# Moving the D parts of the hidden tiles beside the second layer, and splitting half of w2 earlier in the second group

## The chip, the cores and the metric

The kernel runs on one core of one Trainium2 chip. The metric is the device time of one execution in microseconds (us).

## The reference

The kernel computes a gated linear recurrence, and feeds its result to four small networks (experts) whose outputs are mixed with given probabilities.

```python
# q, k, v, alpha: (4, 8, 768, 48)
for t in range(S):
    state = alpha[:, :, t, :, None] * state + einsum('bhd,bhe->bhde', k[:, :, t], v[:, :, t])
    y[:, :, t] = einsum('bhd,bhde->bhe', q[:, :, t], state)
x = y.transpose(0, 2, 1, 3).reshape(3072, 384)
p = domain_probs / (domain_probs.sum(-1, keepdims=True) + 1e-09)     # (3072, 4)
for e in range(4):
    h = maximum(x @ w1[e], 0)            # w1: (4, 384, 1024)
    out += p[:, e:e + 1] * (h @ w2[e])   # w2: (4, 1024, 384)
```

All inputs and outputs are float32.

## The kernel before

**Blocks and groups.** The 3072 rows are 24 blocks of 128 rows. Group 0 has two blocks, groups 1 to 5 have four each, group 6 has two. The blocks' recurrence ("attention" below) is computed chunk by chunk on all engines, in small steps; the expert networks of a group run on TensorE meanwhile. The main loop runs over (group, expert) pairs; in the end groups 5 and 6 alternate expert by expert. The order of all instructions is written out by hand: each engine takes its own in the order in which the program issues them. The attention steps of a later group are dealt out over the earlier group's work by a clock of estimated costs (`cost`, `advance`, `deal`), so that a group's input is ready a little ahead of its first layer.

**First layer (`up`).** For each of the eight hidden tiles `fc` of an expert, the 128 hidden features of all the group's rows (512 columns, in group 6 256) are computed. From group 1 on, x and w1 are split in three float32r parts: a top part T, a low part L (the rest) and a D part, a fixed combination of T and L. Six matmuls (parts T and L) go to the PSUM tile `one` and three (part D) to `two`. ScalarE scales `one` into `t` (line 551), VectorE adds `two`. In groups 0 and 1 a rectified whole float32 tile is then written (lines 558 and 594). From group 2 on `hidden_parts` makes the three parts of the hidden tile: ScalarE writes T (line 578), VectorE L (line 580), and VectorE D = T/4096 - L (`make_dif`, line 590) in two halves of 256 columns. The first half of D is made at once; the second is put into the queue `later`, and is made in the second layer, one at every fourth step. Tiles are finished one tile late: the T and L of a tile are issued after the next tile's matmuls.

**Second layer (`down`).** For a block (128 columns of the hidden tiles as stationary operand, 384 columns of w2 as moving one) eight hidden tiles are summed in PSUM. In groups 0 and 1 this is done in full float32, one block a turn (line 628, one sum). From group 2 on it is done in parts, two blocks a turn: 48 matmuls a turn, first T and L of tiles 0 to 5 for both blocks, then T and L of tiles 6 and 7, and D last; T and L go to one sum and D to another (line 624), so that a turn takes four PSUM banks. `add_up` (line 658) scales the sums by the block's probability and adds them to `acc`. PSUM's tag "g" has four banks, shared by `one`, `two` and these sums.

**Weights.** In group 0 w1 pieces, and in group 1 w2 pieces, are split by `split_piece` (four pieces an expert; two ScalarE and two VectorE instructions each, lines 224 to 230), and the parts are stored to DRAM (`kept`, line 231, from POOL's queue). Later groups load the parts from there (line 195, SP's queue). In groups 0 and 1 the whole w2 pieces are loaded beside the first layer into unused parts of the hidden tiles (line 215, SP's queue); in group 1 pieces 0 and 1 are loaded at hidden tile 0 and pieces 2 and 3 at tile 2. Group 1's splits are issued during its second layer: `background` takes each piece one step on at every call, in `down` twice a turn, in `up` once a hidden tile.

Of the kernel before, what the change touches and what calls it, by code (L numbers as in the profile page):

```python
# [10 lines left out]
F32 = mybir.dt.float32  # L11
# [9 lines left out]
def kernel(  # L21
# [37 lines left out]
    nc = tc.nc  # L59
# [79 lines left out]
    splitting = []  # L139
    stores = deque()  # L140
    late = deque()
    later = deque()
    shared = {}
    accs = {}

# [6 lines left out]


    split1 = lambda gi, e: gi > 0
    split2 = lambda gi, e: gi > 1
    makes = [lambda gi, e: gi == 0, lambda gi, e: gi == 1]


# [28 lines left out]
    def load_piece(l, i, beside=False):  # L187
        if i >= E * NQ * LAST:
            return
        gi, k = divmod(i, E * NQ)  # L190
        e, c = divmod(k, NQ)
        if (split1, split2)[l](gi, e):
            w = wt[l][i] = wts.tile([P, 3, KC * QF], F32R, name=f"w{l + 1}",
                                    bufs=AHEAD if l == 0 else NQ)
            nc.sync.dma_start(out=w.bitcast(F32), in_=kept[l][k])
            return
        if l == 1 and not beside:
            return
        if l == 0:

            if gi > 0 or e == 0:
                shared[c] = wts.tile([P, 3, KC * QF], F32R, name="w2", bufs=NQ)
            w = shared[c][:, 2 - e % 2 if gi == 0 else 2].bitcast(F32)
        else:

            w = hidden[c][:, 0].rearrange("p f n -> p (f n)")[:, :KC * QF].bitcast(F32)
        wt[l][i] = w
        if l == 0:
            heads = moe_w1[e].rearrange("(h d) f -> h d f", d=D)[:, :, c * QF:(c + 1) * QF]
            w = w.rearrange("p (c f) -> p c f", f=QF)  # L210
            for part in range(2):
                nc.sync.dma_start(out=w[:, part], in_=heads[part * H // 2:(part + 1) * H // 2, :QUAD])
            nc.sync.dma_start(out=w[:, 2], in_=heads[:, QUAD:])
        else:
            nc.sync.dma_start(
                out=w.rearrange("p (c d) -> p c d", d=DM),
                in_=moe_w2[e].rearrange("(c p) d -> p c d", p=P)[:, c * FPQ:(c + 1) * FPQ])

    def split_piece(l, i):
        whole = wt[l][i]  # L220
        w = wts.tile([P, 3, KC * QF], F32R, name=f"w{l + 1}", bufs=AHEAD if l == 0 else NQ)
        top, low, dif = (w[:, part] for part in range(3))

        nc.scalar.activation(out=top, in_=whole, func=ACT.Copy, scale=TRIM)
        yield
        nc.scalar.activation(out=dif, in_=whole, func=ACT.Copy, scale=TRIM * 4096)
        yield
        nc.vector.scalar_tensor_tensor(out=low, in0=whole, scalar=4096.0, in1=dif.bitcast(F32),
                                       op0=ALU.mult, op1=ALU.subtract)
        nc.vector.tensor_sub(dif, low.bitcast(F32), top.bitcast(F32))  # L230
        nc.gpsimd.dma_start(out=kept[l][i % (E * NQ)], in_=w.bitcast(F32))
        if l == 0:
            del wt[0][i]

    def background():

# [266 lines left out]
    def up(gi, e, fc, slots=None):  # L503
# [5 lines left out]
        if fc == 0 and begins:  # L509
            for k in range(NQ):  # L510
                hidden[k] = hid.tile([P, 3, FPQ, NT], F32R, name="hT", bufs=NQ)
        if fc in ((0, 2) if gi == 1 else (0,)) and begins and not split2(gi, e):
            half = range(fc, fc + 2) if gi == 1 else range(NQ)
            for k in half:
                load_piece(1, (gi * E + e) * NQ + k, beside=True)
        if makes[0](gi, e) and ends and fc in SPLIT_AT[e in (0, E - 1)]:
            k = SPLIT_AT[e in (0, E - 1)].index(fc)
            making.append(split_piece(0, (gi * E + e) * NQ + k))
# [11 lines left out]
        if not split1(gi, e):  # L530
            for kc in range(KC):
                nc.tensor.matmul(one, lhsT=w[:, kc], rhs=xraws[gi][:, kc, lo:hi],  # L532
                                 start=(kc == 0), stop=(kc == KC - 1))
            nc.scalar.activation(out=whole, in_=one, func=ACT.Relu)
        else:
            two = ps.tile([P, NT], F32, name="two", tag="g", bufs=4)[:, :n]
            for out, terms in ((one, (1, 0)), (two, (2,))):
                for part in terms:
                    for kc in range(KC):
                        nc.tensor.matmul(out, lhsT=w[:, part, kc], rhs=x_part(gi, part, kc),  # L540
                                         start=(part == terms[0] and kc == 0),
                                         stop=(part == terms[-1] and kc == KC - 1))

            ends_first = gi < LAST
            for steps in finish:
                for _ in steps if ends_first else [next(steps)]:
                    pass
            ahead = [] if ends_first else list(finish)
            finish.clear()
            t = work.tile([P, NT], F32, name="t")[:, :n]  # L550
            nc.scalar.activation(out=t, in_=one, func=ACT.Copy, scale=FINE)  # L551
            if split2(gi, e):
                nc.vector.tensor_add(t, t, two)  # L553
                for steps in ahead:
                    next(steps, None)
                finish.append(hidden_parts(t, parts))
            else:
                nc.vector.tensor_add(whole, t, two)  # L558
                finish.append(rectified(whole))
# [16 lines left out]
    def hidden_parts(x, parts):  # L576
        top, low, dif = parts
        nc.scalar.activation(out=top, in_=x, func=ACT.Relu, scale=TRIM)  # L578
        yield
        nc.vector.scalar_tensor_tensor(out=low, in0=x, scalar=0.0, in1=top.bitcast(F32),  # L580
                                       op0=ALU.max, op1=ALU.subtract)

        n = x.shape[-1]
        at = n // 2 if n == NT else 0
        if at:
            make_dif(*(part[:, :at] for part in parts))
        later.append([part[:, at:] for part in parts])

    def make_dif(top, low, dif):
        nc.vector.scalar_tensor_tensor(out=dif, in0=top.bitcast(F32), scalar=1 / 4096.0,  # L590
                                       in1=low.bitcast(F32), op0=ALU.mult, op1=ALU.subtract)
# [5 lines left out]
    def down(gi, e, slots, between):  # L597
# [2 lines left out]
        first = first_piece(gi, e)  # L600
        halves_ = split2(gi, e)
        if slots[0] == 0 and makes[1](gi, e):
            making.extend(split_piece(1, first + k) for k in range(NQ))
        if slots[0] == 0 and makes[0](gi, e) and 0 < e < E - 1:
            making.extend(split_piece(0, first + k) for k in range(2, NQ))
        sums = [[ps.tile([P, DM], F32, name=f"ops{j}", tag="g", bufs=4)
                 for j in range(2 if halves_ else 1)] for _ in slots]

        kinds = [((0, 1), range(FCH - 2)), ((0, 1), range(FCH - 2, FCH)), ((2,), range(FCH))]
        steps = [(part, i, fc) for parts, tiles in (kinds if halves_ else [((3,), range(FCH))])  # L610
                 for part in parts for i in range(len(slots)) for fc in tiles]
        for n, (part, i, fc) in enumerate(steps):
            c, f = divmod(fc, FPQ)
            h = hidden[c][:, :, f, slots[i] * P:(slots[i] + 1) * P]
            advance(cost(1, gi, e) / FCH / (3 if halves_ else 1))
            while between and n >= between[0][0] * len(steps):
                between.popleft()[1]()
            if n == len(steps) // 2:
                background()
            if later and n % 4 == 3:  # L620
                make_dif(*later.popleft())
            if halves_:
                w = wt[1][first + c].rearrange("p t (c d) -> p t c d", d=DM)[:, part, f]
                nc.tensor.matmul(sums[i][part // 2], lhsT=h[:, part], rhs=w,  # L624
                                 start=(fc == 0 and part != 1), stop=(fc == FCH - 1 and part != 0))
            else:
                w = wt[1][first + c].rearrange("p (c d) -> p c d", d=DM)[:, f]
                nc.tensor.matmul(sums[i][0], lhsT=h[:, 2].bitcast(F32), rhs=w,  # L628
                                 start=(fc == 0), stop=(fc == FCH - 1))
            if part >= 1 and fc == FCH - 1:  # L630
                add_up(gi, e, slots[i], part // 2, sums[i][part // 2 if halves_ else 0])
        while between:
            between.popleft()[1]()
        background()
# [35 lines left out]
    def cost(layer, gi, e):  # L670
        n = len(groups[gi]) / 4
        if layer == 0:
            return 2.1 * n if split1(gi, e) else 2.6 * n
        return 4.1 if split2(gi, e) else 5.4

    def deal():

# [29 lines left out]
    def advance(spent):  # L707
        nonlocal clock
        clock += spent
        while waiting and clock >= waiting[0][0]:  # L710
            next(waiting.popleft()[2], None)
# [96 lines left out]
```

## Time and profile before

| | |
|---|---|
| time, median of 3 runs | 1072.71 us (1072.09 to 1073.56) |
| the profiled execution's own time | 1073.32 us |
| its span in the profile | 1071.6 us |
| granted TensorE clock | 0.998 of full speed |
| busy: PE, PEld, DVE, ACT, POOL | 98%, 84%, 72%, 53%, 3% |

PE is TensorE's matmuls, PEld its weight loads, DVE is VectorE, ACT ScalarE, POOL GpSimd; SP issues most of the DMAs. The stages lie in the span as follows (read off the timeline of TensorE, start of the first layer and of the second):

| stage | first layer from | second layer from | next from |
|---|---|---|---|
| group 1, expert 0 | 165.4 | 187.6 | 215.9 |
| group 1, expert 1 | 215.9 | 236.9 | 261.3 |
| group 1, expert 2 | 261.3 | 283.3 | 306.7 |
| group 1, expert 3 | 306.7 | 329.0 | 352.4 |
| group 2, expert 0 | 352.4 | 374.8 | 394.2 |
| group 4, expert 3 | 818.9 | 841.8 | 862.0 |
| group 5, expert 1 | 914.6 | 931.1 | 948.1 |
| group 6, expert 1 | 948.1 | 957.1 | 965.5 |

The rows of the profile's views are explained where they are shown.

### The profile page before, as it was taken

How to read it: one execution, taken by the hardware profiler on the slowest of the kernel's cores; microseconds unless marked ns; L12 is line 12 of the kernel's file. 1: busy time of each engine (PE TensorE's matmuls, PEld its weight loads, DVE VectorE, ACT ScalarE, POOL GpSimd, SP SyncE). 2: the span in 40 equal slices, each digit the busy share in tenths (PEclk: the TensorE clock that was granted, in tenths of full speed). 3: DMA queues.
4: the chain of work that ended last, by engine and by line, in shares of the span. 5: the costliest groups of instructions: out<-in, count | busy, mean ns of one | idle time of the engine just before them, and what ended most of it. 6: DMA issues, size and time to landing. Idle time of an engine off the chain costs nothing.

```text
span 1071.6 us, 21614 instructions
## 1 busy us (share of the span) xinstructions
PE 1048.1 (98%) x8460; PEld 899.1 (84%) x8460; DVE 775.2 (72%) x1711; ACT 566.7 (53%) x1202; POOL 32.7 (3%) x71
## 2 busy tenths in 40 slices
PE   8899999999999999999999999999999999999998
PEld 8777777676776798898898898898889889898988
DVE  5488776656566978778877777986787866666565
ACT  5687866575656554536546445555464543323232
POOL 2010000000000100000000000000000000000000
PEclk9999999999999999999999999999999999999999
DMA  8597699687696967758759558586594543544540
GB/s 123 156 330 216 230 328 368 238 328 241 236 309 209 402 216 274 281 160 312 268 170 359 204 187 337 186 281 234 158 358 173 221 192 147 207 177 178 187 181 31
DMA packets 158838, 251.67 MB, mean 235 GB/s; under 512 B 120112, under 2 KB 135344, under 8 KB 136208
## 3 DMA queue, kind: packets, MB, share of 16 engines
q1 hardware_dynamic: 149600, 208.82, 57.1%
q0 software_dynamic: 5760, 41.29, 9.8%
q8 instruction: 67, 1.10, 0.4%
q10 hardware_dynamic: 3376, 0.17, 0.3%
q14 instruction: 35, 0.29, 0.1%
HBM read 207.79 MB, written 42.47 MB: 234 GB/s over the span
## 4 chain that ended last, share of the span: by engine, by line
PE 83%; DVE 8%; ACT 6%; issue 2%; DMA 1%; SPq 0%; DVEq 0%; ACTq 0%
PE ops L624 25%; PE one L540 21%; PE ops L628 10%; PE two L540 10%; PE sc L334 6%; PE yps L428 3%; PE tp L266 3%; PE one L532 2%; ACT qb L308 2%; PE far L389 1%; PE sps L463 1%; DVE near L344 1%; DVE t L553 1%; DVE hT L580 1%; DVE hT L590 1%
## 5 line engine op out<-in xcount | busy, mean ns | idle before, releaser
L624 PE MATMUL ops<-w,hT 128*128 128x384 f32 x1728 | 318.0, 339 | 4.4 <-DVE acc L658 4.3
L624 PEld LDWEIGHTS ops<-w,hT 128*128 128x128 f32 x1728 | 299.1, 188 | 9.9 <-DVE acc L658 5.6
L540 PE MATMUL one<-xT,w 128*128 128x512 f32 x960 | 253.8, 400 | 2.6 <-DVE xT L248 1.1
L540 PEld LDWEIGHTS one<-xT,w 128*128 128x128 f32 x960 | 176.3, 188 | 41.8 <-DVE QT L315 1.6
L551 ACT ACTIVATE t<-one 128x512 f32<-128x512 f32 (+1 forms) x192 | 106.3, 554 | 153.6 <-PE one L540 148.5
L308 ACT COPY qb<-QT 64x256 f32<-64x256 f32 x336 | 136.4, 406 | 77.0 <-DVE QT L289 44.1
L578 ACT ACTIVATE hT<-t 128x512 fp32r<-128x512 f32 (+1 forms) x160 | 94.3, 589 | 123.6 <-DVE t L553 122.9
L580 DVE SCALAR_TENSOR_TENSOR hT<-t,hT 128x512 fp32r<-128x512 f32 (+1 forms) x160 | 102.2, 638 | 55.7 <-ACT hT L578 53.6
L540 PE MATMUL two<-xT,w 128*128 128x512 f32 x480 | 136.7, 393 | 0.0
L628 PE MATMUL ops<-hT 128*128 128x384 f32 x384 | 133.4, 491 | 0.0
L553 DVE TENSOR_TENSOR t<-t,two 128x512 f32<-128x512 f32 (+1 forms) x160 | 100.8, 630 | 41.9 <-ACT t L551 21.4
L590 DVE SCALAR_TENSOR_TENSOR hT<-hT 128x256 fp32r<-128x256 f32 x288 | 111.9, 422 | 4.4
L540 PEld LDWEIGHTS two<-xT,w 128*128 128x128 f32 x480 | 90.6, 189 | 20.0
L628 PEld LDWEIGHTS ops<-hT 128*128 128x128 f32 x384 | 69.5, 190 | 40.1 <-issue 0.4
L315 DVE TENSOR_TENSOR QT<-QT,dec 128x256 f32<-128x256 f32 x144 | 60.8, 422 | 38.2 <-ACT qb L308 37.5
L344 DVE COPY_PREDICATED near<-masks,sc 128x256 f32<-128x256 uint8 x144 | 77.0, 535 | 15.5 <-PE sc L334 12.8
L334 PEld LDWEIGHTS sc<-qb,KT 128*64 128x64 f32 x2304 | 72.7, 138 | 9.7 <-issue 5.6
L334 PE MATMUL sc<-qb,KT 128*64 128x64 f32 x2304 | 77.2, 223 | 2.6 <-ACT qb L308 2.6
L658 DVE SCALAR_TENSOR_TENSOR acc<-ops,p_all,acc 128x384 f32<-128x384 f32 x82 | 49.5, 614 | 33.9 <-PE ops L624 14.5
L326 ACT COPY KT<-KT 128x256 f32<-128x256 f32 x144 | 59.9, 416 | 3.2
L327 DVE TENSOR_TENSOR KT<-KT,dec 128x256 f32<-128x256 f32 x144 | 60.3, 419 | 0.0
L558 DVE TENSOR_TENSOR hT<-t,two 128x512 f32<-128x512 f32 x32 | 22.0, 688 | 35.6 <-ACT t L551 23.0
(88 smaller groups left out, 970.7 us busy)
## 6 DMA issues: line engine op xcount, KB each, us to landing
w<-kept SPq DMA_DIRECT2D x144, 1152.0 KB
kept<-w POOLq DMA_DIRECT2D x32, 1152.0 KB, 7.4
hT<-in_moe_w_dram SPq DMA_DIRECT2D x32, 384.0 KB
w<-in_moe_w_dram SPq DMA_DIRECT2D x48, 128.0 KB
ra<-in_alpha_dram SPq DMA_DIRECT2D x23, 192.0 KB
rk<-in_k_dram SPq DMA_DIRECT2D x23, 192.0 KB
rq<-in_q_dram SPq DMA_DIRECT2D x23, 192.0 KB
out_dram<-acc POOLq DMA_DIRECT2D x18, 192.0 KB, 6.6
```

What stands on the lines that cost most here:

```text
L308: nc.scalar.copy(out=qb[rows, :, i, :].rearrange("p a (b r) -> p a b r", r=m), in_=qv[rows])
L315: nc.vector.tensor_mul(qv, qv, spread(dv[:, :, :, 0], m))
L334: nc.tensor.matmul(out[HALF * s:HALF * (s + 1), 2 * p:2 * p + 2, :], lhsT=KTs[li][:, p, HALF * s:HALF * (s + 1)], rhs=qbs[li][:, p, :, QUA ...
L344: nc.vector.copy_predicated(near.rearrange("p a (b two r) -> p a b two r", two=2, r=m)[:, :, :, 1, :], mk.unsqueeze(1).broadcast_to([P, H, ...
L540: nc.tensor.matmul(out, lhsT=w[:, part, kc], rhs=x_part(gi, part, kc), start=(part == terms[0] and kc == 0), stop=(part == terms[-1] and k ...
L551: nc.scalar.activation(out=t, in_=one, func=ACT.Copy, scale=FINE)
L553: nc.vector.tensor_add(t, t, two)
L578: nc.scalar.activation(out=top, in_=x, func=ACT.Relu, scale=TRIM)
L580: nc.vector.scalar_tensor_tensor(out=low, in0=x, scalar=0.0, in1=top.bitcast(F32), op0=ALU.max, op1=ALU.subtract)
L590: nc.vector.scalar_tensor_tensor(out=dif, in0=top.bitcast(F32), scalar=1 / 4096.0, in1=low.bitcast(F32), op0=ALU.mult, op1=ALU.subtract)
L624: nc.tensor.matmul(sums[i][part // 2], lhsT=h[:, part], rhs=w, start=(fc == 0 and part != 1), stop=(fc == FCH - 1 and part != 0))
L628: nc.tensor.matmul(sums[i][0], lhsT=h[:, 2].bitcast(F32), rhs=w, start=(fc == 0), stop=(fc == FCH - 1))
```

## The change

It has two parts.

In groups 2 to 5 `hidden_parts` no longer makes the first half of D: both halves (of 256 columns, two blocks) go to queues, `later[0]` for blocks 0 and 1, `later[1]` for blocks 2 and 3, and each turn of the second layer makes the halves that belong to its own two blocks, one at every fourth step. Group 6, whose tiles are one half wide, does this before the change too.

In group 1, experts 1 to 3, the first half of w2 (pieces 0 and 1, hidden tiles 0 to 3) is used in parts: the two pieces are loaded into other parts of the hidden tiles, split during the first layer (put on at tiles 2 and 4), kept in SBUF for the second layer as well as stored, and hidden tiles 0 to 3 are made as three parts. The second layer of these experts then runs two blocks a turn in 32 steps: T and L of tiles 0 to 3, the full float32 matmuls of tiles 4 to 7, and D of tiles 0 to 3, which goes to the same sum as the full ones. Pieces 2 and 3 are split in the second layer as before. Expert 0 of group 1 is unchanged. The cost that the clock takes for these second layers is 4.7 a block where it was 5.4.

```diff
-    later = deque()
+    later = [deque(), deque()]
...
-    split2 = lambda gi, e: gi > 1
+    split2 = lambda gi, e, c=0: gi > 1 or gi == 1 and e > 0 and c < NQ // 2
...
-        if (split1, split2)[l](gi, e):
+        if gi > l:
             w = wt[l][i] = wts.tile(...)
...
-            w = hidden[c][:, 0].rearrange("p f n -> p (f n)")[:, :KC * QF].bitcast(F32)
+            place = (hidden[c][:, 0] if not split2(gi, e, c) else hidden[c + NQ // 2][:, 1])
+            w = place.rearrange("p f n -> p (f n)")[:, :KC * QF].bitcast(F32)
...
         if l == 0:
             del wt[0][i]
+        elif split2(1, *divmod(i - E * NQ, NQ)):
+            wt[1][i] = w
...
-        if fc in ((0, 2) if gi == 1 else (0,)) and begins and not split2(gi, e):
+        if fc in ((0, 2) if gi == 1 else (0,)) and begins and gi < 2:
...
+        if gi == 1 and e > 0 and fc in (2, 4):
+            making.append(split_piece(1, first_piece(gi, e) + fc // 2 - 1))
...
-            if split2(gi, e):
+            if split2(gi, e, c):
...
-        n = x.shape[-1]
-        at = n // 2 if n == NT else 0
-        if at:
-            make_dif(*(part[:, :at] for part in parts))
-        later.append([part[:, at:] for part in parts])
+        for k in range(0, x.shape[-1], 2 * P):
+            later[k // (2 * P)].append([part[:, k:k + 2 * P] for part in parts])
...
-            making.extend(split_piece(1, first + k) for k in range(NQ))
+            making.extend(split_piece(1, first + k) for k in range(NQ // 2 if halves_ else 0, NQ))
...
+        if not halves_:
+            kinds = [((3,), range(FCH))]
+        elif gi == 1:
+            kinds = [((0, 1), range(FCH // 2)), ((3,), range(FCH // 2, FCH)), ((2,), range(FCH // 2))]
...
-            if later and n % 4 == 3:
-                make_dif(*later.popleft())
+            dif = later[slots[0] // 2]
+            if dif and n % 4 == 3:
+                make_dif(*dif.popleft())
...
+            nc.tensor.matmul(sums[i][side], lhsT=h, rhs=w, start=(n in firsts), stop=(n in lasts))
+            if n in lasts:
+                add_up(gi, e, slots[i], part // 2, sums[i][side])
...
-        return 4.1 if split2(gi, e) else 5.4
+        return 4.1 if gi > 1 else 4.7 if split2(gi, e) else 5.4
```

More of the change, by code (lines that the diff above doesn't have):

```diff
@@ L609, in down @@
         kinds = [((0, 1), range(FCH - 2)), ((0, 1), range(FCH - 2, FCH)), ((2,), range(FCH))]
-        steps = [(part, i, fc) for parts, tiles in (kinds if halves_ else [((3,), range(FCH))])
+        if not halves_:
+            kinds = [((3,), range(FCH))]
+        elif gi == 1:
+            kinds = [((0, 1), range(FCH // 2)), ((3,), range(FCH // 2, FCH)), ((2,), range(FCH // 2))]
+        steps = [(part, i, fc) for parts, tiles in kinds
                  for part in parts for i in range(len(slots)) for fc in tiles]
+        sides = [[s for s, step in enumerate(steps) if (step[0] // 2 if halves_ else 0, step[1]) == key]
+                 for key in ((side, i) for i in range(len(slots)) for side in range(len(sums[0])))]
+        firsts, lasts = {s[0] for s in sides}, {s[-1] for s in sides}
         for n, (part, i, fc) in enumerate(steps):
@@ L614, in down @@
             h = hidden[c][:, :, f, slots[i] * P:(slots[i] + 1) * P]
-            advance(cost(1, gi, e) / FCH / (3 if halves_ else 1))
+            advance(cost(1, gi, e) * len(slots) / len(steps))
             while between and n >= between[0][0] * len(steps):
@@ L619, in down @@
                 background()
-            if later and n % 4 == 3:
-                make_dif(*later.popleft())
-            if halves_:
+            dif = later[slots[0] // 2]
+            if dif and n % 4 == 3:
+                make_dif(*dif.popleft())
+            side = part // 2 if halves_ else 0
+            if part < 3:
                 w = wt[1][first + c].rearrange("p t (c d) -> p t c d", d=DM)[:, part, f]
-                nc.tensor.matmul(sums[i][part // 2], lhsT=h[:, part], rhs=w,
-                                 start=(fc == 0 and part != 1), stop=(fc == FCH - 1 and part != 0))
+                h = h[:, part]
             else:
                 w = wt[1][first + c].rearrange("p (c d) -> p c d", d=DM)[:, f]
[L628 to L631, printed above, removed]
+                h = h[:, 2].bitcast(F32)
+            nc.tensor.matmul(sums[i][side], lhsT=h, rhs=w, start=(n in firsts), stop=(n in lasts))
+            if n in lasts:
+                add_up(gi, e, slots[i], part // 2, sums[i][side])
         while between:
```

## The prediction

> **What bounds the kernel now.** I read the page's part 1 first, then TensorE's own waits, then the busy time by stage, and last the order in time of the engines around the first layer's end. The page and the list of TensorE's waits (engine, line, what it waited for; us in total, times, longest):
> ```profile
> PE 1048.1 (98%) x8460; PEld 899.1 (84%) x8460; DVE 775.2 (72%) x1711; ACT 566.7 (53%) x1202; POOL 32.7 (3%) x71
> ...
> PE ops L624 <- DVE acc L658: 4.3, 4, 1.9
> PE far L389 <- ACT qb L308: 3.1, 3, 1.6
> PE yps L428 <- ACT lat L406: 3.1, 4, 1.5
> ```
> TensorE is the bound, and it hardly waits: 23.5 us of 1071.6 are idle, and in groups 2 to 5 only 4.3 us wait for VectorE, at the start of a second turn, when the sums of the first have not left their banks. So time can be won by fewer TensorE cycles (group 1), and lost by making TensorE wait where it doesn't now. Busy time by stage (length; PE, PEld, DVE, ACT):
> ```profile
> 215.90:236.90 21.00, 21.00 (x198) 17.32 (x196) 11.15 (x23) 16.08 (x34) 0.00 (x0) 1.00 0.98 374
> 329.00:352.40 23.40, 23.40 (x118) 14.55 (x116) 17.93 (x35) 16.21 (x33) 1.59 (x3) 1.00 0.68 232
> 818.90:841.80 22.90, 22.42 (x234) 18.18 (x234) 18.26 (x40) 15.07 (x32) 0.00 (x0) 1.00 0.88 358
> 841.80:862.00 20.20, 18.77 (x137) 18.13 (x136) 17.03 (x40) 6.20 (x15) 1.32 (x3) 1.00 0.23 80
> ```
> The reader is to see that VectorE is busy 80% and more in both layers of groups 2 to 4 (the last two rows), and that group 1 (the first two) has room in its first layer. Group 5, where attention is over, shows the chain of one hidden tile bare (start, length):
> ```profile
> 921.86 0.68 DVE L553 TENSOR_TENSOR t<-t,two 128x512 f32<-128x512 f32 x1
> 923.24 0.69 DVE L580 SCALAR_TENSOR_TENSOR hT<-t,hT 128x512 fp32r<-128x512 f32 x1 [0.70 <-ACT hT L578]
> 923.96 0.42 DVE L590 SCALAR_TENSOR_TENSOR hT<-hT 128x256 fp32r<-128x256 f32 x1
> 924.30 0.68 DVE L553 TENSOR_TENSOR t<-t,two 128x512 f32<-128x512 f32 x1
> ```
> The chain repeats after 2.44 us (921.86 to 924.30), of which the half D takes 0.34; TensorE needs 2.06 for a tile (926.98 to 929.04). So VectorE ends the layer about 3 us late, which today costs nothing. The worst case with attention beside it, group 4's last expert:
> ```profile
> 841.77 8.64 PE L624 MATMUL ops<-w,hT 128*128 128x384 f32 x48
> 851.84 2.74 PE L624 MATMUL ops<-w,hT 128*128 128x384 f32 x14 [1.43 <-DVE acc L658]
> ...
> 842.86 0.68 DVE L553 TENSOR_TENSOR t<-t,two 128x512 f32<-128x512 f32 x1
> 844.24 0.69 DVE L580 SCALAR_TENSOR_TENSOR hT<-t,hT 128x512 fp32r<-128x512 f32 x1 [0.70 <-ACT hT L578]
> 844.97 0.42 DVE L590 SCALAR_TENSOR_TENSOR hT<-hT 128x256 fp32r<-128x256 f32 x1
> 846.52 0.43 DVE L315 TENSOR_TENSOR QT<-QT,dec 128x256 f32<-128x256 f32 x1 [1.12 <-ACT qb L308]
> 848.08 1.42 DVE L590 SCALAR_TENSOR_TENSOR hT<-hT 128x256 fp32r<-128x256 f32 x4
> 850.17 1.09 DVE L590 SCALAR_TENSOR_TENSOR hT<-hT 128x256 fp32r<-128x256 f32 x3
> 851.70 0.42 DVE L590 SCALAR_TENSOR_TENSOR hT<-hT 128x256 fp32r<-128x256 f32 x1
> ```
> The 48 matmuls of the first turn run at 0.177 us; the one that would read the eighth D of this turn is number 40, at 841.77 + 39 x 0.177 = 848.7. The eighth D ends at 852.1: 3.5 us late. Today these D are for the second turn, so nobody waits.
>
> **What the Trainium skill says.** "TensorE: Matmul & The Clock Gate", section on the array's architectural detail: VectorE and ScalarE run their queues strictly in order, TensorE reorders weight loads only. The trace agrees: at 846.52 VectorE waits 1.12 us for a ScalarE copy while D work with all inputs ready stands behind. "FP8 and Floating Point Precision", TensorE Precision Notes: true fp32 takes four passes. The trace shows two instructions of 0.323 us a tile against 0.177 for one reduced pass: 3.65 to 1. "VectorE: DVE Perf Modes", on the TRN2 errata: a fixed cost for each instruction; the trace agrees (256 columns 0.42, 512 columns 0.69), so D in halves stays as dear when it moves.
>
> **The change part by part.**
>
> 1. Group 1, experts 1 to 3: 3 experts x 4 blocks x 4 hidden tiles = 48 full-precision tiles become three reduced matmuls each. From the timeline of the second layer, 16 instructions of L628 take 5.33 us, so a tile costs 2 x 0.323 = 0.646; 96 of L624 take 17.15 us, so three cost 3 x 0.177 = 0.531. Saved: 48 x 0.115 = **5.5 us**, all on the path. What it adds lies beside: 12 low parts (0.69) and 24 half D (0.42), 12 more sums (0.61), 26 us of VectorE in all, into the 51 us that it is idle from 215.9 to 352.4 (the sum of the stages' busy times). Two splits (two ScalarE passes of 0.84 and two VectorE of 0.96 a piece) move from the second layer to the first. In expert 1's first layer ScalarE then has 16.1 + 3.4 = 19.5 of 21.0 us. D has room here: asked for at step 15 of 32, read after step 24, with four full tiles (2.6 us) and more between. The pieces' loads go to another place, issued at the same spot of SP's queue; by the trace's packets the first two land in expert 1 at about 220 and 224 us, and their splits are asked for at about 223 and 229. The second of them must now wait until the old piece in its place is split, by my estimate some 2 us after the second layer's end; the load behind it on SP's queue, of w1, is issued 6 us after it today (259.6 to 265.9). POOL's stores stay 16. If ScalarE or a load is late, the activation that frees the banks stands behind it. I charge **0.7 us** (0 to 5).
>
> 2. First half of D, groups 2 to 5, leaves the first layer: 8 x 0.34 = 2.7 us less VectorE there, up to 2.7 us earlier at its end. TensorE was not waiting there, so nothing is gained directly. The second halves leave the first turn for the second, and each turn now asks for its own D. The late one is the eighth: asked for at step 31, read at step 39, 1.4 us on. For each of the 12 second layers of groups 2 to 4, from the timelines as above: start, lateness of the D, and the relief (what fc 7's add lags behind its matmul, at most 2.4, plus 0.34):
>
> 374.8: 1.5, 2.7; 416.3: 2.7, 2.7; 457.6: 0.9, 2.7; 499.8: 1.6, 0.8; 541.3: 1.5, 0.7; 583.0: 2.9, 2.7; 625.2: 2.7, 2.7; 667.1: 2.5, 2.2; 710.4: 2.5, 2.7; 754.6: 3.9, 2.4; 797.0: 0.7, 2.2; 841.8: 3.5, 1.2.
>
> With the full relief the remaining lateness adds up to 5.9 us, with none to 26.9. VectorE's rows between wait for ScalarE copies that partly do not move, so I take three quarters: 0.7 + 1.0 + 1.0 + 0.9 + 0.7 + 0.9 + 0.5 + 2.1 + 2.6 = **10.4 us**. The old waits of **4.3 us** go, since these D waits come ahead of them.
>
> 3. Second turns get 8 x 0.345 = 2.8 us of VectorE work with a deadline. Nine of the twelve have 1 to 4 us idle ahead of the deadline, and all enter with less backlog. Of the other three, two add up the second turn's first sum 0.9 and 2.3 us after its last matmul today (499.8 and 667.1): I put their waits at 1.5 and 2.0. With something off for the relief I charge **3.0 us** (0 to 8).
>
> 4. Group 5 and group 6: group 6 has this form today (its tiles are one half wide), and its eighth D ends 0.4 us before it is read. Group 5's D is 1.6 us late and gains 2.7. Zero; the cover is the absence of attention.
>
> Sum: -5.5 + 0.7 + 10.4 + 3.0 - 4.3 = +4.3 us. The profiled execution took 1073.3 us (span 1071.6 and 1.7 around it), 0.6 over the median of 1072.7. So 1077.0 as a median.
>
> **The rivals.** *Full relief* (faster): D is hardly late, since the ScalarE copies in the chain move with VectorE: 5.9 becomes 2 or less, the second turns cost nothing: -5.5 + 0.7 + 2 - 4.3 = -7, 1066. For it: the copies wait for VectorE in turn (L308 on L315, 27 us). Against: nine of the twelve stages have a lateness over their relief or within 0.3 us of it. It decides where all D waits stay under 7 us (at 9.1 the sum is zero). *Balance*: 5.9 and 3.0 as computed, 1073: no change. *Second bound* (slower still): no relief, 26.9 us less some overlap, or ScalarE late in group 1 with its 5 us: 1072.7 - 5.5 + 5 + 20 - 4.3 = 1088. That the change doesn't act is excluded: the changed program's second layer has 1872 reduced matmuls and 144 full ones where it had 1728 and 192.
>
> **How the numbers follow.** About 0.2% (2.1 us) can be told from no change. Slower 0.60: the sum, and the second bound with 0.12 of it. Faster 0.22, the full relief. Balance 0.18. The range takes in the rival of 1066 and stops short of 1088: 1065.5 to 1086; the slower case alone spans 1075 to 1086.
>
> **What would show it.** Right: TensorE waits for D (the row that makes hT from hT) or the sum behind it in the second layers of groups 2 to 4, 10 us or more in all, near number 33 to 40 of a turn; group 1's second layers of experts 1 to 3 shorter by 1.8 us each; group 5 stages unchanged at 16.5 and 17.0; VectorE's first layer idle more. Wrong: fewer than 5 us of such waits (then faster), or TensorE waiting in group 1's first layer for ScalarE or a load.

## The result, and the profile after

The changed kernel takes 1084.38 us (median of 4 runs, 1082.93 to 1087.45) against 1073.13 us of the kernel before in the same comparison: 1.0109 times as long, 95% interval 1.0084 to 1.0134. It is slower by 11 us. The profiled execution took 1082.93 us (span 1081.1), 9.6 more than that of before.

TensorE's busy time and what it waited for (us in total, times, longest), the same views as before; line 640 holds all matmuls of the second layer now, and line 592 makes D:

```profile
PE 1049.9 (97%) x8508; PEld 905.6 (84%) x8508; DVE 792.7 (73%) x1759; ACT 568.9 (53%) x1202; POOL 32.9 (3%) x71
...
PE ops L640 <- DVE hT L592: 11.9, 23, 1.5
PE yps L431 <- ACT lat L409: 3.1, 4, 1.5
PE far L392 <- ACT qb L311: 3.0, 2, 1.6
```

The row that waited for `acc` (4.3 us) is gone, and its place is taken by 23 waits for D. The list counts only gaps that a reader of the trace can see; a matmul that starts a little late hides in the modelled end of the one before (the thirty-third below starts 0.31 us late, and 0.16 is shown). So I also took from TensorE's rows, for the second layers of groups 2 to 4, how much later than 0.177 us after its predecessor (or after the attention matmuls between them) each matmul starts:

| second layers of groups 2 to 4 (12 stages, 24 turns) | before | after |
|---|---|---|
| first turns, matmuls 33 to 48 (those that read D) | 0.9 us | 16.0 us |
| second turns, matmuls 33 to 48 | 0.2 us | 6.8 us |
| second turns, up to matmul 32 | 6.9 us | 1.7 us |
| first turns, up to matmul 32 | 1.8 us | 1.8 us |

The lengths of the stages, from the start of one layer to the start of the next on TensorE, agree (us):

| | group 0 | group 1, expert 0 | group 1, experts 1 to 3 | groups 2 to 4, first layers | groups 2 to 4, second layers | groups 5 and 6 |
|---|---|---|---|---|---|---|
| before | 138.9 | 50.5 | 136.5 | 264.9 | 244.7 | 205.7 |
| after | 139.6 | 48.8 | 131.2 | 263.9 | 261.4 | 205.8 |

Group 1 gains 5.3 us, the second layers of groups 2 to 4 lose 16.7, and where attention is over nothing changes. (Group 0 and the first expert of group 1 have the same matmuls in all the kernels of this study and vary by up to 3 us between profiled executions, 187.9 to 190.7 together; the experiments below are therefore compared by stage too.)

Busy time by stage, of two second layers and a first one that answer to the rows of before shown in the prediction (stretch of the span, its length, then busy time of PE, PEld, DVE and ACT with the number of instructions): group 1 expert 3's second layer, then both layers of group 4 expert 3.

```profile
324.30:346.10 21.80, 21.80 (x133) 17.08 (x132) 19.50 (x44) 12.64 (x27) 0.00 (x0) 1.00 0.49 164
826.50:849.30 22.80, 22.42 (x235) 18.18 (x233) 16.63 (x34) 15.01 (x32) 0.00 (x0) 1.00 0.88 360
849.30:871.40 22.10, 20.46 (x137) 18.20 (x136) 18.37 (x44) 6.23 (x15) 1.33 (x3) 1.00 0.21 73
```

VectorE has 1.6 us less in the first layer of group 4 (18.26 to 16.63) and 1.3 more in the second (17.03 to 18.37). That second layer is 1.9 us longer, though VectorE is idle in it for 3.7 us: it is not too busy, it is late. TensorE in this stage, in order of time (start, length, and the idle time before with what ended it):

```profile
849.30 5.82 PE L640 MATMUL ops<-w,hT 128*128 128x384 f32 x32
855.27 1.45 PE L640 MATMUL ops<-w,hT 128*128 128x384 f32 x4 [0.16 <-DVE hT L592]
857.36 1.11 PE L640 MATMUL ops<-w,hT 128*128 128x384 f32 x3 [0.65 <-DVE hT L592]
858.89 4.26 PE L640 MATMUL ops<-w,hT 128*128 128x384 f32 x23 [0.42 <-DVE hT L592]
```

The 32 matmuls of parts T and L run through; the 33rd waits for the first D, the 37th for the fifth, the 40th for the eighth. VectorE in the same microseconds:

```profile
853.23 0.43 DVE L318 TENSOR_TENSOR QT<-QT,dec 128x256 f32<-128x256 f32 x1 [1.58 <-ACT qb L311]
...
854.80 1.42 DVE L592 SCALAR_TENSOR_TENSOR hT<-hT 128x256 fp32r<-128x256 f32 x4
856.14 0.42 DVE L318 TENSOR_TENSOR QT<-QT,dec 128x256 f32<-128x256 f32 x1
...
856.89 1.09 DVE L592 SCALAR_TENSOR_TENSOR hT<-hT 128x256 fp32r<-128x256 f32 x3
857.89 0.61 DVE L669 SCALAR_TENSOR_TENSOR acc<-ops,p_fine,acc 128x384 f32<-128x384 f32 x1
858.42 0.41 DVE L592 SCALAR_TENSOR_TENSOR hT<-hT 128x256 fp32r<-128x256 f32 x1
```

VectorE stood idle for 1.58 us for a ScalarE copy of attention before the first D, had other attention rows to do between the fourth and the fifth, and a sum (line 669) between the seventh and the eighth. Each of TensorE's three waits has its row here. The sum stands ahead of the last one, of 0.42 us. It is not alone in that: in 11 of the list's 23 waits a sum stands directly ahead of the D that was waited for, and 8 of these 11 show this same 0.42.

### The profile page after: what moved, and what is told of

Its sections match the earlier page's. It is cut to its first block, busy times and chain, and to the rows that moved or that the text cites. A ratio compares the mean times of both kernels' runs of the same rounds, so it can differ in the third digit from the quotient of the medians.

```text
span 1081.1 us, 21708 instructions
## 1 busy us (share of the span) xinstructions
PE 1049.9 (97%) x8508; PEld 905.6 (84%) x8508; DVE 792.7 (73%) x1759; ACT 568.9 (53%) x1202; POOL 32.9 (3%) x71
## 4 chain that ended last, share of the span: by engine, by line
PE 49%; DVE 12%; ACT 3%; issue 1%; DVEq 0%; ACTq 0%
PE ops L640 20%; PE one L545 15%; PE two L545 7%; PE sc L337 3%; DVE hT L592 3%; PE yps L431 2%; DVE t L558 2%; DVE hT L585 1%; DVE near L347 1%; ACT hT L583 1%; PE tp L269 1%; DVE QT L318 1%; ACT qb L311 1%; DVE KT L330 1%; DVE acc L669 1%
## 5 line engine op out<-in xcount | busy, mean ns | idle before, releaser
L640 PE MATMUL ops<-w,hT 128*128 128x384 f32 x1872 | 357.2, 343 | 12.2 <-DVE hT L592 11.9
L640 PEld LDWEIGHTS ops<-w,hT 128*128 128x128 f32 x1872 | 324.6, 188 | 27.4 <-DVE hT L592 19.8
L585 DVE SCALAR_TENSOR_TENSOR hT<-t,hT 128x512 fp32r<-128x512 f32 (+1 forms) x172 | 110.6, 643 | 66.7 <-ACT hT L583 64.6
L558 DVE TENSOR_TENSOR t<-t,two 128x512 f32<-128x512 f32 (+1 forms) x172 | 109.4, 636 | 59.4 <-ACT t L556 30.8
L583 ACT ACTIVATE hT<-t 128x512 fp32r<-128x512 f32 (+1 forms) x172 | 101.8, 592 | 87.7 <-DVE t L558 86.6
L592 DVE SCALAR_TENSOR_TENSOR hT<-hT 128x256 fp32r<-128x256 f32 x312 | 114.6, 418 | 0.0
L640 PE MATMUL ops<-hT 128*128 128x384 f32 x288 | 100.9, 491 | 0.0
L318 DVE TENSOR_TENSOR QT<-QT,dec 128x256 f32<-128x256 f32 x144 | 60.9, 423 | 36.3 <-ACT qb L311 35.3
L640 PEld LDWEIGHTS ops<-hT 128*128 128x128 f32 x288 | 52.1, 190 | 29.3 <-DMA hT<-in_moe_w_dram 0.6
L669 DVE SCALAR_TENSOR_TENSOR acc<-ops,p_fine,acc 128x384 f32<-128x384 f32 x60 | 36.8, 613 | 13.9 <-PE ops L640 13.8
```

The lines of the kernel that those rows point to most:

```text
L318: nc.vector.tensor_mul(qv, qv, spread(dv[:, :, :, 0], m))
L640: nc.tensor.matmul(sums[i][side], lhsT=h, rhs=w, start=(n in firsts), stop=(n in lasts))
L669: nc.vector.scalar_tensor_tensor(out=acc, in0=part, scalar=scale, in1=acc, op0=ALU.mult, op1=ALU.add)
```

## The experiments

**Theory:** the change has two independent parts. Group 1 gains its TensorE time; the D parts lose because they are asked for too shortly before they are read (the first 29 steps, the eighth only 8 steps of 0.177 us), on a queue whose rows ahead of them (attention, sums) wait for others. **Rivals:** group 1 gives its gain back through ScalarE or the loads; the loss needs the attention steps that the new cost shifts; VectorE simply has too much to do in the second layer.

### Group 1's part alone

The changed kernel, but from group 2 on D is placed as before:

```diff
...
+        if gi > 1 and x.shape[-1] == NT:
+            make_dif(*(part[:, :2 * P] for part in parts))
+            later[0].append([part[:, 2 * P:] for part in parts])
+            return
         for k in range(0, x.shape[-1], 2 * P):
             later[k // (2 * P)].append([part[:, k:k + 2 * P] for part in parts])
```

> The changed kernel with the D parts of groups 2 to 5 as they were before (first half at once, second half in the first turn); only the second group's part of the change is left. Theory (the loss is all D waits in groups 2 to 4, group 1 gains 5.3 us as its stages show): 1068 us, 5 under the kernel before, and TensorE's old waits for the sums of 4 us are back. Rival (group 1 gives part of it back through ScalarE or the loads): 1072 or more.

Measured: 1067.24 us, 0.9942 of the kernel before (0.9923 to 0.9961). Group 1's experts 1 to 3 take 131.0 us against 136.5, groups 2 to 4's second layers 245.2 as before (244.7), and the old wait is back:

```profile
PE ops L644 <- DVE acc L673: 4.4, 4, 1.9
```

The first rival falls: group 1 keeps its gain. In the changed kernel too TensorE's list holds no wait for ScalarE or a load in experts 1 to 3.

### The D parts alone

The kernel before with only the D parts moved:

```diff
-        at = n // 2 if n == NT else 0
-        if at:
-            make_dif(*(part[:, :at] for part in parts))
-        later.append([part[:, at:] for part in parts])
+        for k in range(0, x.shape[-1], 2 * P):
+            later[k // (2 * P)].append([part[:, k:k + 2 * P] for part in parts])
...
-            if later and n % 4 == 3:
-                make_dif(*later.popleft())
+            dif = later[slots[0] // 2]
+            if dif and n % 4 == 3:
+                make_dif(*dif.popleft())
```

> The kernel before with the D parts moved as in the change, group 1 untouched. Theory: the stages of groups 2 to 4 grow by 16 us net, so 1089 us, with 20 us and more of D waits. Rival (the loss needs the attention steps that the new cost of 4.7 shifts): under 1080.

Measured: 1087.40 us, 1.0134 (1.0110 to 1.0157). The second layers of groups 2 to 4 take 258.9 us; the matmuls that read D start 14.7 us late in the first turns and 6.3 in the second.

```profile
PE ops L622 <- DVE hT L587: 11.7, 20, 1.7
```

So the loss is there without the new cost of 4.7: the second rival falls as its cause. The two parts roughly add up: 0.9942 and 1.0134 give 1.0076, against 1.0109 measured together, and the intervals meet. By the stages the second layers of groups 2 to 4 lose 14.2 us here and 16.7 in the changed kernel; what makes the difference of 2.5 stays open, and the attention steps that the new cost shifts may have a part in it.

### D asked for early

The changed kernel with the same D instructions, each asked for sooner (the first 31 steps before it is read, the eighth 24):

```diff
-            if dif and n % 4 == 3:
+            if dif and n % (2 if gi > 1 else 4) == (1 if gi > 1 else 3):
```

> The changed kernel with D asked for at every second step from step 1 (1, 3, ... 15) in groups 2 to 6, not at every fourth (3, 7, ... 31); the same work. Theory (a D asked for 8 steps before it is read stands behind attention rows and the sum on VectorE's queue): 15 to 20 of the 23 us of D waits go, 1065 to 1069. Rival (the amount of VectorE work in the second layer decides, not its place): 1080 or more.

Measured: 1068.14 us, 0.9943 (0.9925 to 0.9962). This is the decisive run: VectorE does the same work in the same layer, and 16 us are gone. The second layers of groups 2 to 4 take 245.1 us. D waits that stand in the list of TensorE's waits fall from 11.9 us to 0.5; by the late starts 5.0 us are left in first turns and 0.2 in second ones. The rival that VectorE has too much to do falls. The time is that of group 1's part alone, so the move no longer costs anything, but it doesn't gain either. In group 4's last second layer all eight D of the first turn now run together, ahead of the attention rows that stood between them:

```profile
840.89 0.43 DVE L318 TENSOR_TENSOR QT<-QT,dec 128x256 f32<-128x256 f32 x1 [1.58 <-ACT qb L311]
...
842.46 2.76 DVE L592 SCALAR_TENSOR_TENSOR hT<-hT 128x256 fp32r<-128x256 f32 x8
845.14 0.42 DVE L318 TENSOR_TENSOR QT<-QT,dec 128x256 f32<-128x256 f32 x1
```

The wait for the ScalarE copy ahead of them is still there, and in this stage the first D comes 0.3 us late behind it. Another 1.1 us comes from the D rows themselves: eight of them take 2.76 us, and TensorE would read them in 8 x 0.177 = 1.4.

### D ahead of the sum

Only two steps earlier, so that the eighth D comes before the first sum:

```diff
-            if dif and n % 4 == 3:
+            if dif and n % 4 == (1 if gi > 1 else 3):
```

> The changed kernel with D asked for at steps 1, 5, ... 29 of a turn, not 3, 7, ... 31, in groups 2 to 6: the eighth D then stands ahead of the first sum on VectorE, and each D two steps (0.35 us) earlier. Theory (the eighth D is late by what stands ahead of it in the queue): 0.5 us off each of the some 14 late turns of the changed kernel, 1077 to 1080 against its 1084. Rival (VectorE as a whole is behind, the order of two rows changes nothing): 1083 and more.

Measured: 1075.62 us, 1.0017 (1.0009 to 1.0026), more than was expected of it: 8.8 us off the changed kernel by the medians. The late starts go from 16.0 to 9.7 us in first turns and from 6.8 to 5.0 in second ones, 8.1 together.

```profile
PE ops L640 <- DVE hT L592: 5.1, 9, 1.2
```

This run moved two things at once, the sum and 0.35 us for each D, and doesn't divide the 8.1 us between them. It shows how steep the cost is in the place of an instruction on the queue.

### The second half alone in the second turn

First half at once, as before; second half asked for in the second turn:

```diff
...
+        if gi > 1 and x.shape[-1] == NT:
+            make_dif(*(part[:, :2 * P] for part in parts))
+            later[1].append([part[:, 2 * P:] for part in parts])
+            return
```

> The changed kernel, but in groups 2 to 5 the first half of D is made at once as before, and only the second half is made in the second turn. Theory: the 16 us of D waits of first turns go, the 7 us of second turns stay or grow a little as VectorE is no longer relieved in the first layer, and the first turn's sums find nothing ahead of them: 1069 to 1071. Rival (VectorE has too much to do in the second layer as a whole): as much as half of the loss stays, 1076 and more.

Measured: 1073.47 us, 0.9994 (0.9983 to 1.0005): neither theory's number nor the rival's. The D waits of first turns are gone (0.7 us) and those of second turns are 8.8, as expected. What I missed is the waits for banks at the start of second turns: 3.6 us of late starts are left of group1_alone's 7.3, although no D stands ahead of the first turn's sums any more. With VectorE unrelieved in the first layer, attention rows alone can hold up the sums; the next run shows a stage of it.

### Towards a better place

Three more kernels keep group 1's part and look for a better place for D. First, the kernel of the last section with D asked for at steps 1, 3, ... 15 of the second turn:

```diff
...
-            if dif and n % 4 == 3:
+            if dif and (n % 2 == 1 if gi > 1 and len(groups[gi]) > 2 else n % 4 == 3):
```

> The changed kernel, but in groups 2 to 5 the first half of D is made at once as before, and the second half in the second turn at its steps 1, 3, ... 15. Theory (a D that is asked for a whole 17 steps or more before it is read is on time, and without D ahead of them the first turn's sums leave their banks in time): group1_alone's 1067 less the 5 to 6 us of its second turns' waits, 1061 to 1063. Rival (D early in the second turn holds up the attention rows behind it, or the last sums, as much): 1066 and more.

Measured: 1066.29 us, 0.9935 (0.9922 to 0.9947). D waits are gone (0.4 us), second layers of groups 2 to 4 take 242.7, 2.5 less than in group1_alone; the 3.6 us of late starts at the head of second turns stay, as in the run before, so the expected 1061 to 1063 was not reached. The time is the one that the rival named, but its mechanism isn't seen: nothing is lost in place of the D waits. (Of the 2.5 us that the stages gain, the time shows about 1: group 0 and the first expert of group 1 took 2.5 us longer in this profiled execution than in group1_alone's.) In group 4's expert 1 the first turn's sums stand behind attention rows that waited for ScalarE, with no D among them:

```profile
757.95 0.43 DVE L318 TENSOR_TENSOR QT<-QT,dec 128x256 f32<-128x256 f32 x1 [1.48 <-ACT qb L311]
...
758.76 1.14 DVE L673 SCALAR_TENSOR_TENSOR acc<-ops,p_fine,acc 128x384 f32<-128x384 f32 x2
```

TensorE, whose first turn's last matmul starts at 757.52, starts the second turn at 759.43.

Second, with the first half again made at once, four tiles' second halves in the first turn and four in the second:

```diff
...
+            both = gi > 1 and len(groups[gi]) > 2
-            dif = later[slots[0] // 2]
-            if dif and n % 4 == 3:
+            dif = later[0 if both else slots[0] // 2]
+            if dif and (n in ((3, 7, 11, 15), (0, 2, 4, 6))[slots[0] // 2] if both else n % 4 == 3):
```

> The changed kernel, but in groups 2 to 5 the first half of D is made at once, and of the second half four tiles are made in the first turn (steps 3, 7, 11, 15) and four in the second (steps 0, 2, 4, 6). Theory: the first turn's sums have four D fewer ahead of them, and so lose at least half of their 5 to 6 us of waits; the four early ones in the second turn are on time: 1062 to 1065. Rival: 1067, as with all eight in the first turn.

Measured: 1065.66 us, 0.9931 (0.9918 to 0.9945), not to be told from the one before; second layers of groups 2 to 4 take 242.8 us. The late starts at the head of second turns are 4.4 us of 7.3; 2.9 are saved, where at least half was expected.

Third, second_turn_early with the first halves of tiles 4 to 7 moved too, asked for at steps 1, 3, 5 and 7 of the first turn, 32 steps and more before they are read:

```diff
...
-        if gi > 1 and x.shape[-1] == NT:
+        if gi > 1 and x.shape[-1] == NT and fc < FCH // 2:
```

> second_turn_early, with the first halves of D of hidden tiles 4 to 7 moved from the first layer into the first turn, at its steps 1, 3, 5 and 7. Theory (a relief at the end of the first layer lets VectorE reach the first turn's sums earlier, and D asked for 25 steps ahead is on time): the 3.6 us that TensorE still loses in second_turn_early's second turns ahead of D shrink to some 2.5, with under 1 us of D waits: its second layers of groups 2 to 4 at 241 to 242 us in place of 242.7, 1064 to 1066 in all. Rival (the relief is used up by waits for ScalarE as in the changed kernel, and the four D in the first turn delay its sums): 243 us and more, 1067 or more.

Measured: 1062.88 us, 0.9904 (0.9888 to 0.9921), somewhat better than expected and the fastest of the study: 1% under the kernel before, and faster than the changed kernel by 21 us. Second layers of groups 2 to 4 take 240.1 us; the late starts at D are 1.2 us in both turns together, those at the start of second turns 2.4. Neither D nor a sum is left among the first rows of TensorE's waits:

```profile
PE yps L431 <- ACT lat L409: 3.1, 4, 1.5
PE far L392 <- ACT qb L311: 3.0, 2, 1.6
PE sc L337 <- ACT qb L311: 2.6, 3, 1.2
PE one L545 <- DVE xT L251: 1.4, 2, 0.8
```

So the idea of moving D beside the second layer was sound in part: a relief at the end of the first layer is worth something, if what is moved is asked for in time.

## Why the prediction was right, and where its size was off

The forecast was slower, with 1077 as the number; the time is 1084, inside the range, near its upper end: the loss is 11 us where 4 were forecast. By its steps, all in us of the profiled execution:

| step | predicted | measured |
|---|---|---|
| group 1, experts 1 to 3 | -5.5 + 0.7 | -5.3 |
| D waits of first turns | +10.4 | +15.1 (16.0 for 0.9) |
| D waits of second turns | +3.0 | +6.6 (6.8 for 0.2) |
| old waits for banks | -4.3 | -5.2 (1.7 for 6.9) |
| groups 5 and 6 | 0 | +0.1 |
| the rest (first layers, group 0, group 1's expert 0) | 0 | -2.0 |

**Right:** group 1's price, from two paces on the timeline of before, and that ScalarE and the loads would not undo it. Right too: that D would be late only where attention runs, that the wait would stand at matmuls 33 to 40, that the banks' waits would go, and that groups 5 and 6 would not move.

**The mis-sized term: the relief.** The prediction let VectorE reach the end of the first layer up to 2.7 us earlier in a stage, 25.7 us over the twelve, and used three quarters of it, 19.3, against the lateness. What came shows at the eighth D of the first turn: counted from the start of the second layer, it ends on average 10.2 us in before and 8.9 after, 14.5 us earlier over the twelve stages. Most of what is missing was missing already at the end of the first layer. There the end of the eighth tile's L lies on average 4.1 us after the start of the second layer in before (49.1 over the twelve stages) and 3.0 after (36.3). That is 12.8 us, where the prediction's list without its 0.34 for the D behind that L had 21.6.

In group 5 the full 2.7 came from expert 1 on (5.07 to 2.35). Why not in groups 2 to 4? VectorE's rows of group 5's expert 0 after show a piece in which it is behind (start, length):

```profile
876.19 0.68 DVE L558 TENSOR_TENSOR t<-t,two 128x512 f32<-128x512 f32 x1
877.57 0.69 DVE L585 SCALAR_TENSOR_TENSOR hT<-t,hT 128x512 fp32r<-128x512 f32 x1 [0.70 <-ACT hT L583]
878.17 0.68 DVE L558 TENSOR_TENSOR t<-t,two 128x512 f32<-128x512 f32 x1
```

Without D the chain of a tile takes 1.98 us against TensorE's 2.06. It no longer falls behind, but it catches up by less than 0.1 us a tile (on these tiles and the next its additions start 0.46, 0.39 and 0.31 us after the last matmul of their tile ends). So where attention rows have made VectorE late within the layer, nearly all of that lateness stays to its end: in six of the twelve stages the last tile's addition still starts 1.5 to 1.8 us after the start of the second layer, where 0.3 is the figure of a stage without lateness.

With the shifts of the eighth D's end in place of the computed ones, the prediction's list of lateness gives about 12.5 us for first turns, where 10.4 were charged. That is not quite half of the 4.7 us by which first turns were priced too low. Another 1.3 us are in one stage (group 2, expert 2), for which the list had nothing left: the fortieth matmul came late there in before already, behind attention's matmuls, and now waits for D instead. The rest is spread over the stages, and its cause stays open.

**Second turns** were charged 3.0 us: 1.5 and 2.0 for two stages (the last experts of groups 2 and 3), with something off for the relief. These two measure 4.0 (1.3 and 2.7). The other 2.8 are in stages that were put at nothing, most of them in experts 1 and 3 of group 4 (1.3 and 0.7) and expert 1 of group 2 (0.6). That the smaller relief is behind this too is argued; no run measured it by itself. What second_half_in_second_turn adds is that with no relief at all second turns cost 8.8.

**The rivals.** "Full relief" (1066) and "balance" needed more relief than came. "Second bound" (1088) had the right direction for the D waits, but group 1 kept its gain. The sum between the seventh and the eighth D stood there in before too, and so is contained in the lateness that was read; it was not priced apart.

## What to carry to other kernels

On an engine that works in order, work that is moved costs nothing only if it is asked for so early that a delay ahead of it does no harm: before moving a producer next to its consumer, count the rows that will stand ahead of it, and what each of them waits for. A relief further up is worth its length only where the engine can catch up; compare the period of its chain with that of the engine it follows. Here the moved D parts lost 1.3% by themselves; with half of the first halves left in place and every moved one asked for 24 steps or more ahead, moving gained 0.4% beyond group 1's own 0.6%.

## What the runs showed of the hardware that I had not expected

- The chain without D, two VectorE instructions of 0.69 us with one of ScalarE between them, takes 1.98 us a tile (876.19 to 878.17 above), and VectorE stands idle for 0.70 of that: the way over ScalarE, not VectorE's work, sets the period.
- Leaving the half D out of this chain shortened it by 0.46 us (2.44 to 1.98), though the row behind a D starts 0.34 us after it, which is what the prediction took. The D reads what the L ahead of it writes, and starts 0.72 us after it (923.24 to 923.96 in the prediction's lines); the addition doesn't, and starts 0.60 after it (877.57 to 878.17).
- Eight D in a row take 2.76 us, 0.345 each, where one alone is shown with 0.42: their lengths in the profile overlap, so a sum over rows overstates VectorE's work.
